# Attention, a 2-D Fourier mix and a feed-forward net on one core: the second feature chunk is made 97 wide, and the last 64 keys are weighed in four 64x64 tiles

## The chip, the core and the metric

The program runs on one core of a Trainium2 chip. It works on five engines: TensorE (PE in the profile, with its weight loads as PEld), VectorE (DVE), ScalarE (ACT), GpSimd (POOL), and SyncE (SP), whose queue issues the DMAs. The metric is the device time of one execution in microseconds.

## The reference

Attention over 4 batches, 12 heads, 448 tokens and 64 features a head, with a soft cap; then the real part of a 2-D Fourier transform over tokens and features is added; then a layer norm and a two-layer net of 768 to 3072 to 768.

```
scores = scale * q @ k.T;  scores = cap * tanh(scores / cap)
attn   = exp(scores - max) / (sum + 1e-9);  x = attn @ v        # heads side by side: 4 x 448 x 768
u      = x + real(fft(fft(x, axis=1), axis=2))
un     = (u - mean(u)) / sqrt(var(u) + 1e-6)
out    = u + maximum(un @ w_ch1, 0) @ w_ch2
```

Everything is computed with the accuracy of 32-bit floats. Operands of the net and of the scores are split into a head and a rest, so that each product is three matmuls of the type fp32r. The products with the values `v` and the transform use plain 32-bit matmuls. In the trace a plain 32-bit matmul is two records, and an fp32r matmul is one.

## The kernel before

**Attention** goes by pairs of heads: 6 pairs in each of 4 batches, 24 in all. The 448 keys of a pair are cut into 7 units: three chunks of 128 keys for head 0, three for head 1, and one unit that holds the last 64 keys of head 0 on partitions 0 to 63 and the last 64 keys of head 1 on partitions 64 to 127. I call that one the shared unit. It is the last unit of an even pair and the first of an odd one (`chunk`, L366), so there are 24 shared units among 168, and two of them always meet at the border of two pairs.

Two units make a tile `t`. `scores` (L398) computes k times q for both units, keys on the partitions and 452 query columns, into one of two PSUM tiles. The units of one head use 64 rows of the array, and those of the other head use the other 64. `tanh` and `exp` (L413, L417) run on ACT over 128x904 elements, from PSUM into one of five SBUF tiles `a`.

`weigh` (L423) multiplies the exponentials with the values. Queries stand in four groups of 112 to 114, and each group is cut at 64, so a unit of one head is 8 matmuls: keys on 128 rows, 64 or 50 query columns as the stationary operand, and 65 moving columns (64 features and a column of ones that gives the denominator). For the shared unit the moving operand is 130 wide: `vt` holds two chunks for it (numbers 7 and 8) with head 0's values beside zeros and zeros beside head 1's. PSUM tile `av` has two banks. Groups 0 and 1 are in the first, groups 2 and 3 in the second. There is one `av` tile only, so a pair's first `weigh` waits until DVE has read the pair before it (`denominators`, `normalise`, L445 and L454).

**The transform** of a batch runs when its six pairs are there. DVE folds the tokens and the features. 193 folded features remain; they are cut into 97 and 96 (`FW`, L55). `stage1` (L498) transforms over tokens: for each feature chunk `p` and each half `sd` 8 matmuls, whose stationary operand has 64 columns and then 33 (`p` = 0) or 32 (`p` = 1), and whose output goes to partitions 0 to 63 and from 64 on. `combine` copies on ACT and adds on DVE into `y`. `stage2` (L528) transforms over features, with 97 or 96 rows.

**The net** takes the 24 groups of 128 hidden channels two by two: `up` (L739) and `down` (L762), all on TensorE with 448 columns, three matmuls for each product.

**What sets the order.** Every step has a place in a table (`ORDER`, L91), and the steps are recorded in that order. Each engine runs its own steps strictly so. The table interleaves the attention of later pairs with the transform of earlier batches. The net can't begin in full before the last `tanh`, whose PSUM tiles it takes over (L955 to L959).

## Time and profile before

| what | value |
|---|---|
| time, median of 3 runs | 955.84 us (955.51 to 956.01) |
| the profiled execution's own time | 956.33 us |
| its span, first to last instruction | 954.1 us |
| PE busy | 939.2 us, 98% |
| DVE busy | 733.6 us, 77% |
| ACT busy | 362.3 us, 38% |
| granted TensorE clock | 1.000 |

The 2.2 us between the span and the execution's own time lie around the program. The profiled execution is 0.49 us above the median. A page of the profile gives busy shares over the whole span; since the first quarter (attention and transform) and the rest (the net) are different programs, the shares have to be read by stage. Busy time of PE counts a matmul from its start to a modelled end, and such records overlap, so the pitch from one start to the next is the cost of a matmul and not its mean duration.

### The profile page before, as it was taken

The page shows a single profiled execution, that of the slowest core. Times are in us where ns is not written, and L with a number is a line of the kernel's source. Part 1 is how long each engine was busy: PE and PEld are TensorE (multiplying, and loading weights), DVE is VectorE, ACT ScalarE, POOL GpSimd, SP SyncE. Part 2 cuts the span into 40 slices and gives each one's busy share as a digit, 9 for nine tenths or more (in the row PEclk, how much of TensorE's full clock was granted, in tenths as well). Part 3 has the DMA queues.
Part 4 walks back from the last instruction along what each step waited for, and adds up shares of the span by engine and source line. Part 5 has one row for each costly group of instructions (what it writes and reads, how often), then busy time and mean ns, then how long its engine had stood idle before and what let it go on. Part 6 is the DMA issues. An engine that isn't in the chain of part 4 may idle for free.

```text
span 954.1 us, 17612 instructions
## 1 busy us (share of the span) xinstructions
PE 939.2 (98%) x7264; PEld 834.5 (87%) x7264; DVE 733.6 (77%) x1486; ACT 362.3 (38%) x563; POOL 16.5 (2%) x50
## 2 busy tenths in 40 slices
PE   6999999999999999999999999999999999999998
PEld 5888788787888999999999999999999999999997
DVE  3589887798988887887877878778777777777733
ACT  6998989995431312222122221221212221122100
POOL 0000101000100000000000000000000000000000
PEclk9999999999999999999999999999999999999999
DMA  5454332420021222111221212111211121112023
GB/s 158 124 172 137 103 106 50 126 49 19 11 76 34 67 60 59 58 60 50 62 65 50 60 50 64 53 50 52 64 50 50 50 67 50 50 51 64 18 108 124
DMA packets 51055, 66.17 MB, mean 69 GB/s; under 512 B 30752, under 2 KB 35616, under 8 KB 50976
## 3 DMA queue, kind: packets, MB, share of 16 engines
q1 hardware_dynamic: 50896, 64.81, 22.8%
q8 instruction: 57, 0.93, 0.4%
q10 hardware_dynamic: 80, 0.25, 0.1%
q14 instruction: 22, 0.18, 0.1%
HBM read 59.53 MB, written 5.52 MB: 68 GB/s over the span
## 4 chain that ended last, share of the span: by engine, by line
PE 95%; DVE 2%; ACT 1%; DMA 1%; issue 1%; SPq 0%; DVEq 0%
PE ph L747 37%; PE po L776 36%; PE av L436 9%; PE s L405 7%; PE yps L506 3%; PE pq L534 2%; PE pt L621 1%; DMA qkr<-qkT 1%; ACT a L415 1%; ACT a L418 0%; DVE xc L737 0%; DVE xc L785 0%; ACT hh L758 0%; DVE hh L759 0%; DVE bs L567 0%
## 5 line engine op out<-in xcount | busy, mean ns | idle before, releaser
L776 PE MATMUL po<-hh,w 128*128 128x448 f32 x1728 | 361.8, 367 | 1.8 <-DVE xc L785 1.4
L747 PE MATMUL ph<-xs,w 128*128 128x448 f32 x1728 | 359.3, 366 | 0.0
L776 PEld LDWEIGHTS po<-hh,w 128*128 128x128 f32 x1728 | 323.0, 188 | 34.2 <-DVE xc L785 5.1
L747 PEld LDWEIGHTS ph<-xs,w 128*128 128x128 f32 x1728 | 323.9, 188 | 27.8 <-issue 0.6
L785 DVE TENSOR_TENSOR xc<-xc,po 128x448 f32<-128x448 f32 x288 | 176.7, 618 | 44.4 <-PE po L776 43.9
L666 ACT ACTIVATE wt<-raw 128x384 f32<-128x384 f32 x96 | 53.5, 557 | 243.7 <-DVE w L698 242.4
L759 DVE SCALAR_TENSOR_TENSOR hh<-ph,hh 128x448 fp32r<-128x448 f32 x96 | 60.0, 625 | 96.7 <-ACT hh L758 96.5
L758 ACT ACTIVATE hh<-ph 128x448 fp32r<-128x448 f32 x96 | 52.3, 544 | 170.4 <-PE ph L747 170.4
L436 PEld LDWEIGHTS av<-vt,a 128*50 128x50 f32 (+1 forms) x2688 | 91.4, 131 | 12.4 <-issue 9.1
L436 PE MATMUL av<-vt,a 128*64 128x65 f32 (+3 forms) x2688 | 98.8, 230 | 0.3 <-PE rt L590 0.3
L310 ACT CAST w<-wt 128x384 fp32r<-128x384 f32 x96 | 49.3, 514 | 130.2 <-DVE wt L673 130.2
L418 ACT ACTIVATE a<-a,capt 128x904 f32<-128x904 f32 x84 | 86.1, 1063 | 0.6
L405 PE MATMUL s<-qhl,khl 64*128 64x452 f32 (+1 forms) x504 | 78.1, 400 | 8.2 <-DVE khl L315 7.6
L415 ACT ACTIVATE a<-s,tscale 128x904 f32<-128x904 f32 x84 | 83.5, 1022 | 7.0 <-PE s L405 5.8
L405 PEld LDWEIGHTS s<-qhl,khl 64*128 64x128 f32 (+1 forms) x504 | 51.7, 193 | 21.9 <-DVE khl L315 7.6
L673 DVE SCALAR_TENSOR_TENSOR wt<-wt 128x384 f32<-128x384 f32 x96 | 53.6, 559 | 10.8 <-DVE wt L670 0.9
L670 DVE SCALAR_TENSOR_TENSOR wt<-raw,wt 128x384 uint32<-128x384 uint32 x96 | 53.7, 559 | 3.3
L692 DVE SCALAR_TENSOR_TENSOR wt<-raw,wt 128x384 f32<-128x384 uint32 x96 | 53.6, 558 | 3.3
L698 DVE TENSOR_TENSOR w<-wt 128x384 fp32r<-128x384 f32 x96 | 53.6, 558 | 3.3
L315 DVE TENSOR_TENSOR wt<-wt,w 128x384 f32<-128x384 f32 x96 | 52.9, 551 | 0.7 <-ACT w L310 0.7
L667 DVE TENSOR_SCALAR wt<-raw 128x384 uint32<-128x384 uint32 x96 | 34.2, 356 | 1.3
L689 DVE TENSOR_SCALAR wt<-wt 128x384 uint32<-128x384 uint32 x96 | 34.0, 354 | 0.4
(61 smaller groups left out, 399.5 us busy)
## 6 DMA issues: line engine op xcount, KB each, us to landing
raw<-w2r SPq DMA_DIRECT2D x48, 384.0 KB
raw<-w1r SPq DMA_DIRECT2D x48, 384.0 KB
qkr<-qkT SPq DMA_DIRECT2D x23, 482.0 KB
vt<-vr SPq DMA_DIRECT2D x24, 288.0 KB
outT<-xc SPq DMA_DIRECT2D x24, 224.0 KB
dev<-lnrow SPq DMA_DIRECT2D x4, 224.0 KB
mean<-lnrow SPq DMA_DIRECT2D x4, 224.0 KB
featT<-feat SPq DMA_DIRECT2D x2, 386.0 KB
```

The costliest lines, as they stand in the source:

```text
L405: nc.tensor.matmul(ps_t[t][:, i, :SQ], khl[p % 2][rows, ik, k0 : k0 + P], qhl[p % 2][rows, iq], start=(k_ == 0), stop=(k_ == 2),)
L415: nc.scalar.activation(a_t[t], ps_t.pop(t)[:, :, :SQ], AF.Tanh, scale=tscale)
L418: nc.scalar.activation(a_t[t], a_t[t], AF.Exp, scale=capt)
L436: nc.tensor.matmul(pa_t[p][q0:q1, g // 2, o : o + n_ * (D + 1)], a_t[t][:, n, OFF[g] + q0 : OFF[g] + q1], v, start=u % 7 == 0 and g % 2 == ...
L670: nc.vector.scalar_tensor_tensor(tu, hi.bitcast(U32), 0xC0000000, tu, op0=ALU.bitwise_and, op1=ALU.bitwise_or)
L673: nc.vector.scalar_tensor_tensor(t, w, HI_MIN, t, op0=ALU.is_ge, op1=mul)
L692: nc.vector.scalar_tensor_tensor(w, lo, 2.0**-52, w, op0=mul, op1=mul)
L698: nc.vector.tensor_tensor(ws[c][1][:, sl], t, w, op=add)
L747: nc.tensor.matmul(ph[:, :S], w_[:, dc * P : (dc + 1) * P], x_, start=(k_ == 0), stop=(k_ == 3 * NDC - 1),)
L759: nc.vector.scalar_tensor_tensor(hh[:, 1], ph[:, :S], 0.0, f32(hh[:, 0]), op0=ALU.max, op1=sub)
L776: nc.tensor.matmul(po[:, :S], w_[:, dc * P : (dc + 1) * P], hh[:, x_], start=(k_ == 0), stop=(k_ == 3 * GF - 1),)
L785: nc.vector.tensor_tensor(ac, ac, po[:, :S], op=add)
```

## The change

The feature chunks are both 97 wide. The second starts at feature 96 rather than 97, so feature 96 is in both, and the constant `feat` has zeros for it in the second chunk. `stage1` has 33 columns in its upper half for both chunks, and `combine` and `stage2` work on 97 partitions for both.

The shared unit is weighed head by head. The stationary operand is the head's 64 rows, 64 or 50 columns, and the moving operand is 65 columns of one chunk of `vt` (number 6), of which partitions 0 to 63 belong to head 0 and the others to head 1. That makes 16 matmuls in place of 8. Each head has a PSUM bank of `av` with its four query groups, and the reads of `denominators` and `normalise` follow it. `vt` has 7 chunks in place of 9, so its load is 7/9 as large and three small memsets go.

```
-FW = (NF // 2 + 1, NF // 2)
+FW = NF // 2 + 1
...
-        for p, w in enumerate(FW):
-            d = (p * FW[0] + np.arange(w))[:, None]
-            half = np.where(d == NF - 1, 0.5, 1.0)
+        for p in range(2):
+            d = (p * (NF - FW) + np.arange(FW))[:, None]
+            half = np.where(d == NF - 1, 0.5, 1.0) * np.where((d == NF - FW) & (p == 1), 0.0, 1.0)
...
-    vt = new([P, 2, 9, D + 1], F32, "vt", 1, "vt")
+    vt = new([P, 2, 7, D + 1], F32, "vt", 1, "vt")
...
-        i, n_ = {None: (7, 2), 0: (c + (c > 0), 1), 1: (4 + c, 1)}[head]
-        v = vt[:, p % 2, i : i + n_].rearrange("q a c -> q (a c)")
+        i = 6 if head is None else 3 * head + c
+        first, last = ((0, 1), (6, 6)) if p % 2 == 0 else ((0, 0), (5, 6))
         for g in range(4):
-            o = (g % 2 * 2 + (head or 0)) * (D + 1)
-            for q0, q1 in ((0, D), (D, R)):
-                nc.tensor.matmul(
-                    pa_t[p][q0:q1, g // 2, o : o + n_ * (D + 1)],
-                    a_t[t][:, n, OFF[g] + q0 : OFF[g] + q1],
-                    v,
-                    start=u % 7 == 0 and g % 2 == 0,
-                    stop=u % 7 == 6 and g % 2 == 1,
+            for j in (0, 1) if head is None else (head,):
+                rows = slice(P) if head is not None else slice(j * D, (j + 1) * D)
+                for q0, q1 in ((0, D), (D, R)):
+                    nc.tensor.matmul(
+                        pa_t[p][q0:q1, j, g * (D + 1) : (g + 1) * (D + 1)],
+                        a_t[t][rows, n, OFF[g] + q0 : OFF[g] + q1],
+                        vt[rows, p % 2, i],
+                        start=u % 7 == first[j] and g == 0,
+                        stop=u % 7 == last[j] and g == 3,
...
-        f, p0, w = f_t[b, sd], p * FW[0], FW[p]
+        f, p0 = f_t[b, sd], p * (NF - FW)
...
-                for q0, q1 in ((0, D), (D, w)):
+                for q0, q1 in ((0, D), (D, FW)):
```

The order of the steps is untouched. What changes in TensorE's row of instructions is seen at the end of pair 5, where a shared unit is followed by the first `stage1` of a second chunk (`p` = 1, half 0 of batch 0), then scores, then the shared unit of pair 6. In the rows, `av` is the tile of `weigh`, `yps` that of `stage1` and `s` that of `scores`, and the sizes are stationary by moving columns. Before:

```order
L436 MATMUL av<-vt,a 50x65
L436 MATMUL av<-vt,a 64x130
L436 MATMUL av<-vt,a 50x130
...
L506 MATMUL yps<-seqT,ff 64x113
L506 MATMUL yps<-seqT,ff 32x113
...
L405 MATMUL s<-qhl,khl 128x452 x12
```

The same place on TensorE in the changed kernel:

```order
L434 MATMUL av<-vt,a 64x65
L434 MATMUL av<-vt,a 50x65
...
L504 MATMUL yps<-seqT,ff 64x113
L504 MATMUL yps<-seqT,ff 33x113
...
L402 MATMUL s<-qhl,khl 128x452 x12
```

Nothing stands in another place. The shared unit's 8 rows with 130 columns are 16 rows with 65, and the 8 rows of `stage1` end on 33 columns and no longer on 32.

## Rows read from the trace of the kernel before

**Rows 1.** The page, part 4: the chain that ended last, shares by engine and line.

```profile
PE 95%; DVE 2%; ACT 1%; DMA 1%; issue 1%; SPq 0%; DVEq 0%
PE ph L747 37%; PE po L776 36%; PE av L436 9%; PE s L405 7%; PE yps L506 3%; PE pq L534 2%; PE pt L621 1%; DMA qkr<-qkT 1%; ACT a L415 1%; ACT a L418 0%; DVE xc L737 0%; DVE xc L785 0%; ACT hh L758 0%; DVE hh L759 0%; DVE bs L567 0%
```

**Rows 2.** Busy time of each engine by stretch: attention, last transform, net.

```profile
core 0: us, PE busy (x) PEld busy (x) DVE busy (x) ACT busy (x) POOL busy (x), PEclk, DMA share, GB/s
...
20.00:225.60 205.60, 204.93 (x3525) 168.35 (x3521) 167.32 (x379) 195.33 (x248) 11.62 (x30) 1.00 0.37 104
225.60:300.00 74.40, 71.88 (x425) 60.07 (x426) 63.47 (x126) 24.05 (x47) 3.85 (x10) 1.00 0.10 34
300.00:954.00 654.00, 650.50 (x3186) 596.96 (x3185) 496.37 (x965) 130.99 (x254) 0.00 (x0) 1.00 0.20 59
```

**Rows 3.** Waits of ACT, 20 to 225.6: for whom, total us, times, longest.

```profile
ACT a L415 <- PE s L405: 4.4, 8, 1.4
ACT yh L310 <- PE yps L506: 2.9, 5, 1.3
ACT a L415 <- PE av L436: 1.1, 4, 0.3
ACT khl L310 <- PE s L405: 0.5, 2, 0.3
ACT xc L310 <- PE pt L621: 0.3, 1, 0.3
```

**Rows 4.** PE in order of time, both chunks' `stage1`: start, us, instructions.

```profile
61.70 0.99 PE L506 MATMUL yps<-seqT,ff 112*64 112x113 f32 x16
62.51 2.02 PE L436 MATMUL av<-vt,a 128*50 128x65 f32 x48
64.36 2.61 PE L506 MATMUL yps<-seqT,ff 112*64 112x113 f32 x16
66.91 1.50 PE L405 MATMUL s<-qhl,khl 64*128 64x452 f32 x12
```

**Rows 5.** PE in order of time: `weigh` alone, and with a shared unit.

```profile
24.55 3.01 PE L436 MATMUL av<-vt,a 128*64 128x65 f32 x96
...
152.06 2.08 PE L436 MATMUL av<-vt,a 128*64 128x65 f32 x64
...
205.12 3.90 PE L436 MATMUL av<-vt,a 128*64 128x130 f32 x112
```

**Rows 6.** PE in order of time: scores of two heads, one tile.

```profile
216.01 0.88 PE L405 MATMUL s<-qhl,khl 64*128 64x452 f32 x6
```

**Rows 7.** Forms of `weigh` on PE, all of the span: busy us, mean ns.

```profile
L436 PE MATMUL av<-vt,a 128*64 128x65 f32 x1152 | 75.4, 224 | 0.0
L436 PE MATMUL av<-vt,a 128*64 128x130 f32 x192 | 26.0, 277 | 0.3 <-PE rt L590 0.3
```

**Rows 8.** ACT in order of time around its longest waits (in brackets).

```profile
86.46 1.01 ACT L415 ACTIVATE a<-s,tscale 128x904 f32<-128x904 f32 x1 [1.35 <-PE s L405]
87.38 1.98 ACT L418 ACTIVATE a<-a,capt 128x904 f32<-128x904 f32 x2
...
90.80 1.05 ACT L418 ACTIVATE a<-a,capt 128x904 f32<-128x904 f32 x1
...
121.88 0.59 ACT L310 COPY yh<-yps 96x226 f32<-96x226 f32 x2 [1.29 <-PE yps L506]
...
134.95 1.02 ACT L415 ACTIVATE a<-s,tscale 128x904 f32<-128x904 f32 x1 [0.57 <-PE s L405]
...
147.34 1.01 ACT L415 ACTIVATE a<-s,tscale 128x904 f32<-128x904 f32 x1 [0.79 <-PE s L405]
...
190.95 0.35 ACT L310 COPY yh<-yps 97x226 f32<-97x226 f32 x1 [0.70 <-PE yps L506]
```

**Rows 9.** All engines in order of time: the last pair and the last batch's `stage1`.

```profile
217.49 3.87 PE L436 MATMUL av<-vt,a 128*64 128x130 f32 x112 [0.30 <-PE rt L590]
...
221.42 0.23 DVE L451 TENSOR_SCALAR den<-av,guard 114x8 f32<-114x8 f32 x1 [0.46 <-PE av L436]
...
226.36 0.56 DVE L491 TENSOR_TENSOR ff<-tf 114x386 f32<-114x386 f32 x1
...
227.37 1.03 DVE L491 TENSOR_TENSOR ff<-tf 114x386 f32<-114x386 f32 x2
...
228.38 0.34 ACT L310 COPY yh<-yps 96x226 f32<-96x226 f32 x1 [2.40 <-PE yps L506]
...
228.76 1.77 DVE L526 TENSOR_TENSOR y<-yps,yh 96x226 f32<-96x226 f32 x4 [0.35 <-ACT yh L310]
...
229.71 3.59 PE L506 MATMUL yps<-seqT,ff 112*64 112x113 f32 x32 [0.45 <-ACT yh L310]
...
233.38 0.34 ACT L310 COPY yh<-yps 96x226 f32<-96x226 f32 x1 [1.80 <-issue]
233.76 0.81 DVE L526 TENSOR_TENSOR y<-yps,yh 96x226 f32<-96x226 f32 x2 [1.78 <-ACT yh L310]
...
234.63 1.85 PE L534 MATMUL pq<-featT,y 96*64 96x192 f32 x20 [0.20 <-DVE y L526]
```

More of the change, by code (lines that the diff above doesn't have):

```diff
@@ L256, in _dft_constants @@
     for n, f in enumerate((np.cos, np.sin)):
-        for p, w in enumerate(FW):
-            d = (p * FW[0] + np.arange(w))[:, None]
-            half = np.where(d == NF - 1, 0.5, 1.0)
-            feat[n, :w, p, NJO : NJO + len(j_even)] = half * f(2 * np.pi * ((d * j_even) % DM) / DM)
-            feat[n, :w, p, :NJO] = half * f(2 * np.pi * ((d * j_odd) % DM) / DM)
+        for p in range(2):
+            d = (p * (NF - FW) + np.arange(FW))[:, None]
+            half = np.where(d == NF - 1, 0.5, 1.0) * np.where((d == NF - FW) & (p == 1), 0.0, 1.0)
+            feat[n, :FW, p, NJO : NJO + len(j_even)] = half * f(2 * np.pi * ((d * j_even) % DM) / DM)
+            feat[n, :FW, p, :NJO] = half * f(2 * np.pi * ((d * j_odd) % DM) / DM)
     ks = np.array(KODD + KEVEN)
@@ L429, in weigh @@
             pa_t[p] = psum.tile([P, 2, 512], F32, tag="av", bufs=1, name="av")
-        i, n_ = {None: (7, 2), 0: (c + (c > 0), 1), 1: (4 + c, 1)}[head]
-        v = vt[:, p % 2, i : i + n_].rearrange("q a c -> q (a c)")
+        i = 6 if head is None else 3 * head + c
+        first, last = ((0, 1), (6, 6)) if p % 2 == 0 else ((0, 0), (5, 6))
         for g in range(4):
-            o = (g % 2 * 2 + (head or 0)) * (D + 1)
-            for q0, q1 in ((0, D), (D, R)):
-                nc.tensor.matmul(
-                    pa_t[p][q0:q1, g // 2, o : o + n_ * (D + 1)],
-                    a_t[t][:, n, OFF[g] + q0 : OFF[g] + q1],
-                    v,
-                    start=u % 7 == 0 and g % 2 == 0,
-                    stop=u % 7 == 6 and g % 2 == 1,
-                    skip_group_check=True,
-                )
+            for j in (0, 1) if head is None else (head,):
[7 more added lines that the diff above has]
+                        stop=u % 7 == last[j] and g == 3,
+                        skip_group_check=True,
+                    )
     def denominators(p):
@@ L448, in denominators @@
             u_t[b] = new([P, 4, DM], F32, f"x{b % 2}", 1, "u")
-        pa = pa_t[p][:R, :, : 4 * (D + 1)].rearrange("q a (g c) -> q a g c", g=4)
+        pa = pa_t[p][:R, :, : 4 * (D + 1)].rearrange("q j (g c) -> q j g c", g=4)
         den = den_t[p] = new([P, 2, 4, 1], F32, "den", 2, "den")
@@ L455, in normalise @@
         b, c0 = p // NP, PAIRS[p % NP] * 2 * D
-        pa = pa_t[p][:R, i, : 4 * (D + 1)].rearrange("q (g j c) -> q g j c", g=2, j=2)
-        den = den_t[p][:R, i].rearrange("q (g j) c -> q g j c", g=2)
+        pa = pa_t[p][:R, :, : 4 * (D + 1)].rearrange("q j (g c) -> q g j c", g=4)[:, 2 * i : 2 * i + 2]
+        den = den_t[p][:R, :, 2 * i : 2 * i + 2].rearrange("q j g c -> q g j c")
         nc.vector.tensor_tensor(
             u_t[b][:R, 2 * i : 2 * i + 2, c0 : c0 + 2 * D].rearrange("q g (j c) -> q g j c", j=2),
-            pa[:, :, :, :D],
+            pa[..., :D],
             den.to_broadcast([R, 2, 2, D]),
@@ L518, in combine @@
             y_t[b, p] = new([P, 2, 2 * NT2], F32, "y", 2, "y")
-        y, w = y_t[b, p][: FW[p], sd], FW[p]
-        ps = d_t.pop(("y", b, p, sd))[:w, : 4 * NK].rearrange("w (n e m) -> w n e m", n=2, e=2)
-        half = new([P, 2, NK], F32, "yh", 2, "yh")[:w]
+        y = y_t[b, p][:FW, sd]
+        ps = d_t.pop(("y", b, p, sd))[:FW, : 4 * NK].rearrange("w (n e m) -> w n e m", n=2, e=2)
+        half = new([P, 2, NK], F32, "yh", 2, "yh")[:FW]
         copy("combine", b, half, ps[:, :, 1])
@@ L531, in stage2 @@
         for sd, (j0, nj) in enumerate(SDJ):
-            for p, w in enumerate(FW):
+            for p in range(2):
                 for q0, q1 in ((0, D), (D, R)):
@@ L535, in stage2 @@
                         ps[q0:q1, j0 : j0 + nj],
-                        y_t[b, p][:w, sd, k0 + q0 : k0 + q1],
-                        featT[n][:w, p, j0 : j0 + nj],
+                        y_t[b, p][:FW, sd, k0 + q0 : k0 + q1],
+                        featT[n][:FW, p, j0 : j0 + nj],
                         start=(p == 0),
@@ L973 @@
         qk[:, :, j, :, SQ + P :] = kj[..., : 3 * P]
-    vr = np.zeros((B, NP, P, 9, D), np.float32)
-    chunks = v[:, :, : 3 * P].reshape(B, NP, 6, P, D).transpose(0, 1, 3, 2, 4)
-    vr[:, :, :, 0], vr[:, :, :, 2:7] = chunks[:, :, :, 0], chunks[:, :, :, 1:]
+    vr = np.zeros((B, NP, P, 7, D), np.float32)
+    vr[:, :, :, :6] = v[:, :, : 3 * P].reshape(B, NP, 6, P, D).transpose(0, 1, 3, 2, 4)
     for j in range(2):
-        vr[:, :, j * D : (j + 1) * D, 7 + j] = v[:, j::2, 3 * P :]
+        vr[:, :, j * D : (j + 1) * D, 6] = v[:, j::2, 3 * P :]
     arrays = {
```

3 lines of the change are left out of this document (removed).

## Prediction

> **What bounds the kernel now.** The chain that ended last comes first: 95% of it is PE, with the net's two lines at 73% [rows 1]. The table by stage then tells which part of the program the change can reach. From 300 us on, PE is busy 650.5 of 654 us with `up` and `down`, which the diff doesn't touch [rows 2]. So every gain has to be made before, and is then carried to the end as a shift of the net. From 20 to 225.6 us (attention with the transforms of batches 0 to 2), PE is busy 204.9 of 205.6 us, but ACT is busy 195.3 too [rows 2]. Two engines are nearly full at once, and a saving on PE is worth no more than what ACT loses by waiting for PE. The share of ACT over the whole span, 38%, hides this.
>
> ACT's waits in that stretch are all for PE and sum to 9.2 us in 20 waits (4.4, 2.9, 1.1, 0.5 and 0.3) [rows 3]. Each also costs the overlap of two instructions: two exps in a row take 1.98 us and one alone 1.05, so the second adds 0.93, and 0.12 is lost when ACT has to start afresh [rows 8]. Twenty times 0.1 is 2.0. **ACT's bound is therefore 9.2 + 2.0 = 11.2 us** for the stretch. From 225.6 to 300 us the last batch's transform has chains of its own, below.
>
> **Part 1: 33 columns in place of 32.** The first chunk's `stage1` takes from 61.70 to 62.51 us, 0.81, and the second chunk's from 64.36 to 66.91, 2.55 [rows 4]. Both are 16 records over the same 113 moving columns, and the second has one stationary column fewer. In the first chunk the blocks of 64 and of 33 columns stream side by side in two halves of the array, 8 records each, so one takes 0.81/8 = 0.10 us. One after the other 16 records would take 1.62 us. The second chunk needs 0.93 more than that, and what is left to explain it is that a block of 32 columns is a narrower strip of the array than one of 64, and that the array empties when the strips change: 8 changes in 8 matmuls, 0.93/8 = 0.12 us each. With 33 columns both blocks are of the wider kind, as in the first chunk. Eight such steps (4 batches, 2 halves) save 8 x 1.74 = 13.9 us on PE; six of them, 10.4 us, lie before 225.6 us. The extra row that `combine` and `stage2` get is no extra column for ACT or DVE, and I cost it at nothing: DVE's and ACT's time goes by columns, and `stage2` rows of 97 already stand beside those of 96.
>
> **Part 2: the shared unit.** `weigh` costs (3.01 - 2.08)/32 = 0.029 us a record with 65 columns, from 96 and 64 records, so 0.47 us for a unit of 16 [rows 5]. Six such units and a shared one take 3.90 us, which puts the shared unit at 3.90 - 3.01 = 0.89 [rows 5]. It has 16 records of twice the columns; a record is modelled at 277 ns against 224 [rows 7]. After the change it has 32 records of 65 columns on four tiles of the array. The trace of before shows no fp32 matmul on half of the rows, so I bound it. At best the four tiles stream side by side, and the unit costs what 8 records in each of four tiles cost: 0.47. At worst they share what two tiles have now: 32 x 0.029 = 0.93. The nearest row is the scores: six matmuls, three in each half of the rows, with 452 columns take 0.88 us, and twelve take 1.50, so two of them cost 0.21, about what 452 columns take at one a cycle of 2.4 GHz (0.19) with the clock granted in full [rows 2, 4, 6]. Two halves of the rows do run side by side there, and I take 0.47.
>
> To that come changes between tiles of 128 rows and of 64. Where a shared unit borders on scores there was a change already; where it borders on `weigh`, `stage1` or `stage2` there is a new one. In the program's order I count 26 for 24 units, at 0.12 each: 0.13 a unit. So the unit goes from 0.89 to 0.60, and 23 units (one lies before 20 us) save 23 x 0.29 = 6.7 us.
>
> The Trainium skill, in "TensorE: Matmul & The Clock Gate", section "Wait — 56ns, not 53.3ns?", says that matmuls never start less than some 25 ns apart, however few columns they have. By it 32 records would take an estimated 0.80 us, and with the changes 0.93, so this part would save nothing. The trace has no stretch of `weigh` denser than the 29 ns above, so it doesn't decide; this is the second rival.
>
> The load of `vt` is 7/9 as large; no row of PE waits for it in this stretch, so nothing. `denominators` and `normalise` read the same number of elements from two banks; a read of PSUM that got dearer would lie behind PE's wait for `av`, but I see no reason for it.
>
> **What of it arrives.** PE saves 10.4 + 6.7 = 17.1 us before 225.6, and ACT can gain 11.2. So ACT becomes the bound, and the question is which of its waits close. The five longest make 4.70 of the 9.2 us [rows 8]. The two for `combine` (1.29 and 0.70) stand right behind second-chunk `stage1` and close whole: 1.99. The one at 86.46 (1.35) follows 5 us of `stage2`, `weigh` and scores that don't shrink, and PE's lead from earlier savings is limited by the two PSUM tiles of scores; I give it 1.0. Ahead of those at 134.95 and 147.34 (0.57, 0.79) only shared units shrink, one and two of them: 0.3 + 0.6. Together 3.89 of 4.70, 83%. The same share of 11.2 us is **9.3 us**.
>
> **The end of attention.** The last two pairs' `weigh` each hold a shared unit, and DVE waits for them: at 221.42 for 0.46 us [rows 9]. Each is 0.3 us shorter: **0.6 us**.
>
> **The last batch's `stage1`** stands alone on the chain. The first (second chunk) has its second half's input at 226.36 + 0.56 = 226.92 and its result is copied at 228.38 [rows 9]. Four matmuls, two by two, need 4 records of 0.10 us in each half of the array, so this half would end at 227.4. But the add that follows finds DVE busy with the other fold until 227.37 + 1.03 = 228.40, so it starts at 228.40 and not 228.76: 0.36 is won. The third `stage1` starts when that add has freed its PSUM tile, 229.71 - 0.36 = 229.35, and ends by 230.3 (0.9 later). The fourth, second chunk again, then takes 0.9 us in place of 2.55 and is copied at some 231.25 in place of 233.38. Its adds end at 232.5 (behind the third's, which end at 231.6), against 233.76 + 0.81 = 234.57. `stage2`, at 234.63 on the path, goes on at 232.5 [rows 9]. **2.1 us** of the 3.5 that PE saves.
>
> Behind that PE and DVE go on with the same work, all of it shifted. Sum: 9.3 + 0.6 + 2.1 = **12.0 us**. The profiled execution took 956.33 us, so it would take 944.3; it is 0.49 above the median, and I predict **943.8 us**.
>
> **The rivals.**
>
> *Half of ACT's waits stay.* The order was laid out for PE as slow as it is, and when PE is early it waits for an exp, or for DVE to read the one `av` tile, and ACT then waits for PE's answer. That DVE waits for `av` and PE for DVE in turn speaks for it; that so many waits stand behind work that shrinks by more than they last speaks against it. Half of 11.2 is 5.6: 5.6 + 0.6 + 2.1 = 8.3 us, 947.5.
>
> *The shared unit gains nothing* (four tiles get the issue rate of two, the page's rule above). It would cost 0.93 + 0.13 = 1.06, and 23 of them 3.9 us more than now. PE then saves 10.4 - 3.9 = 6.5 us in the stretch, all of it below ACT's bound; at 83% 5.4 us, nothing at the end of attention, and 2.1: 7.5 us, 948.3.
>
> *Slower: halves of the rows empty the array.* If going from head 0's rows to head 1's costs what a change of strip costs in the second chunk's `stage1` (0.12), the unit has 8 such changes and no overlap of the halves: 0.93 + 0.13 + 8 x 0.12 = 2.0 us, 1.1 above now, and the 23 cost 25.3 us against 10.4 saved. PE, which is full, ends attention 14.9 us later; with 2.1 won after it the kernel takes 968.6. It decides from about 0.54 us more a unit ((10.4 + 2.1)/23). Against it stand the scores, which change halves at every matmul and still overlap [rows 6]. The Trainium skill, "TensorEngine Tiling (Array Packing)", section "Key Properties", says that a change of mode drains TensorE and a change of tile within a mode doesn't; by that this rival is out, and the scores agree.
>
> *ACT isn't the bound* and all of PE's saving arrives: 17.1 + 0.6 + 2.1 = 19.8, 936.0. ACT's busy time speaks against it.
>
> **How the numbers follow.** Chances: the forecast 0.60, half of the waits 0.18, no gain in the shared unit 0.14, slower 0.04, the full saving 0.04. The range is made of the first three. At the fast end all of ACT's 11.2, 0.6, the 2.1 with half a microsecond more, and some 1.5 for waits too short to be listed: 15.9, 939.9, say 939.5. At the slow end the two rivals together: half of 6.5, and 2.1, which is 5.4: 950.4, say 950.5. Faster by over 0.2% (about what a measurement of this kernel can tell from no change) has 0.95, within it 0.01, slower 0.04.
>
> **What the profile of the changed kernel would show.** Every `stage1` of 16 records at 0.8 us; if a second chunk still takes over 2, part 1 is wrong. A shared unit at 0.5 to 0.6 us between its neighbours; 0.9 or more means the second rival. ACT's waits for PE before the last exp down from 9.2 to 2 or 3 us, and visible waits of PE for ACT in their place, which there are hardly any of now; if ACT's waits stay at 5, the first rival. The net's part (from its first full `up` to the end) unchanged within 1 us; if it grew, the shift was lost to DVE or to the weights' loads there, and the prediction is wrong in its last step.

## The result, and the profile after

The changed kernel takes **947.62 us** (median of 5 runs, 945.25 to 950.13) against 955.84 (954.55 to 956.10) for the kernel before on the same chip: a ratio of 0.9916, with a 95% interval of 0.9895 to 0.9938. It is 8.2 us faster; 943.8 and a gain of 12.0 had been forecast. Two things stand out before any row is read. The gain is two thirds of the forecast, and the five runs lie 4.9 us apart where the five of before lay 1.6 apart. The profiled execution took 947.62 us, its span 945.5.

The page's chain that ended last, shares by engine and line, answers [rows 1]:

```profile
PE 83%; ACT 7%; DVE 7%; issue 2%; DMA 0%; POOL 0%; SPq 0%; DVEq 0%; ACTq 0%; POOLq 0%
PE ph L745 37%; PE po L774 37%; PE av L434 4%; PE s L402 3%; ACT a L412 3%; ACT a L415 2%; PE pq L532 2%; DVE y L524 1%; ACT u L610 1%; DVE bs L565 1%; DVE u L456 1%; DMA capt<-cap 0%; ACT xc L310 0%; ACT khl L310 0%; DVE tf L475 0%
```

PE had 95% of the chain and has 83%. The net's two lines are where they were (74%); it is attention that has changed hands, with 7% each for ACT and DVE. The table by stage, for the stretches that answer [rows 2] (each stage begins some 6 to 8 us sooner):

```profile
core 0: us, PE busy (x) PEld busy (x) DVE busy (x) ACT busy (x) POOL busy (x), PEclk, DMA share, GB/s
20.00:219.70 199.70, 190.33 (x3870) 156.17 (x3868) 165.61 (x376) 192.88 (x246) 12.40 (x30) 1.00 0.34 100
219.70:292.20 72.50, 68.35 (x428) 59.25 (x427) 63.31 (x127) 24.29 (x48) 3.83 (x10) 1.00 0.11 35
292.20:945.50 653.30, 649.73 (x3186) 596.74 (x3184) 496.00 (x965) 131.17 (x254) 0.00 (x0) 1.00 0.19 59
```

PE's busy time in attention fell from 204.9 to 190.3 us, and 9.4 us of the stretch are now idle on PE, where 0.7 were. The work was taken off TensorE as planned; a good part of what was taken off became TensorE's waiting. The net is unchanged (649.7 us of PE's time against 650.5).

The waits of ACT in that stretch (whom for, us in total, times, longest), against [rows 3]:

```profile
ACT a L412 <- PE s L402: 2.7, 4, 0.8
ACT wt L664 <- DVE w L696: 1.3, 2, 1.0
ACT a L412 <- PE av L434: 0.9, 2, 0.6
ACT khl L310 <- PE s L402: 0.5, 2, 0.3
ACT yh L310 <- PE yps L504: 0.4, 1, 0.4
ACT xc L310 <- PE pt L619: 0.3, 1, 0.3
```

They sum to 6.1 us, 4.8 of it for PE, where 9.2 stood. Half of ACT's waits for PE stayed, which the prediction had named as the sign of its first rival.

What the two parts do to the instructions themselves is in PE's order of time (start, us, instructions). First both chunks' `stage1`, against [rows 4]:

```profile
62.04 0.99 PE L504 MATMUL yps<-seqT,ff 112*64 112x113 f32 x16
62.85 1.73 PE L434 MATMUL av<-vt,a 128*50 128x65 f32 x64
64.52 0.99 PE L504 MATMUL yps<-seqT,ff 112*64 112x113 f32 x16
65.44 0.88 PE L402 MATMUL s<-qhl,khl 64*128 64x452 f32 x6
```

The first chunk takes 0.81 us to the next instruction, the second 0.92, where it took 2.55. Then the shared unit, alone between scores and `stage2`:

```profile
85.66 0.69 PE L434 MATMUL av<-vt,a 64*64 64x65 f32 x32
86.28 2.83 PE L532 MATMUL pq<-featT,y 97*64 97x194 f32 x32
```

It has 32 records and takes 0.62 us (85.66 to 86.28). 0.60 was forecast; the unit of before, at this same place, took 0.95 (86.97 to 87.92). 0.62 us for 32 records is 19 ns a record. The Trainium skill, in "TensorE: Matmul & The Clock Gate", section "Wait — 56ns, not 53.3ns?", says that matmuls never start less than some 25 ns apart; here, with four tiles of the array in use, they do, and the trace decides.

One row of the changed kernel has no answer in the kernel before:

```profile
51.93 1.15 PE L434 MATMUL av<-vt,a 128*64 128x65 f32 x31
54.80 1.62 PE L434 MATMUL av<-vt,a 128*50 128x65 f32 x49 [1.72 <-issue]
```

In the middle of a `weigh` of 80 records TensorE stands for 1.7 us and waits for no semaphore. Until 54 us this execution was 1.5 us ahead of the profile of before; behind the stop it is 0.3 behind, by VectorE's instructions. Then the lead builds up anew, to 1.9 at 92 us, 3.8 at 156, 5.9 at 222 and 7.9 at 300 (the same instruction's start in both traces, on ACT or DVE); at 600 us it is 8.2.

So three questions go to the chip: what the stop is, what the spread is, and why half of ACT's waits stay although PE has 14.6 us less to do.

### The profile page after: what moved, and what is told of

Same layout as the page of the kernel before. It is cut to its first block, busy times and chain, and to the rows that moved or that the text cites. A ratio compares the mean times of both kernels' runs of the same rounds, so it can differ in the third digit from the quotient of the medians.

```text
span 945.5 us, 18375 instructions
## 1 busy us (share of the span) xinstructions
PE 920.4 (97%) x7648; PEld 821.2 (87%) x7648; DVE 732.4 (77%) x1486; ACT 361.5 (38%) x563; POOL 17.0 (2%) x47
## 4 chain that ended last, share of the span: by engine, by line
PE 83%; ACT 7%; DVE 7%; issue 2%; DMA 0%; POOL 0%; SPq 0%; DVEq 0%; ACTq 0%; POOLq 0%
PE ph L745 37%; PE po L774 37%; PE av L434 4%; PE s L402 3%; ACT a L412 3%; ACT a L415 2%; PE pq L532 2%; DVE y L524 1%; ACT u L610 1%; DVE bs L565 1%; DVE u L456 1%; DMA capt<-cap 0%; ACT xc L310 0%; ACT khl L310 0%; DVE tf L475 0%
## 5 line engine op out<-in xcount | busy, mean ns | idle before, releaser
L434 PEld LDWEIGHTS av<-vt,a 128*50 128x50 f32 (+3 forms) x3072 | 84.4, 130 | 18.3 <-issue 11.0
L434 PE MATMUL av<-vt,a 128*50 128x65 f32 (+3 forms) x3072 | 92.0, 223 | 4.0 <-issue 1.7
L402 PE MATMUL s<-qhl,khl 64*128 64x452 f32 (+1 forms) x504 | 78.5, 399 | 11.2 <-DVE khl L315 8.5
```

Of the source, the lines that this page charges most:

```text
L402: nc.tensor.matmul(ps_t[t][:, i, :SQ], khl[p % 2][rows, ik, k0 : k0 + P], qhl[p % 2][rows, iq], start=(k_ == 0), stop=(k_ == 2),)
L434: nc.tensor.matmul(pa_t[p][q0:q1, j, g * (D + 1) : (g + 1) * (D + 1)], a_t[t][rows, n, OFF[g] + q0 : OFF[g] + q1], vt[rows, p % 2, i], sta ...
```

## Experiments

Twelve more runs follow, the first of them of the changed kernel itself. Each was timed beside the kernel before on the same chip, but not all twelve on one chip; the edits are to the changed kernel unless said otherwise.

**The changed kernel again** (`e1_again`, no edit), to see whether the stop comes again.

> The changed kernel once more, word for word. In its first trace TensorE stands still for 1.9 us at 54.8 us in the middle of a weigh, with no semaphore to wait for, and all the lead it had by then (1.5 us) is gone. Theory A (its instructions came late, because their load stood behind a burst of other DMAs from 48.7 us on): the stop is there again, at the same instruction, with 1 to 2.5 us. Rival (a chance event): no stop there, and the profiled execution is 1.5 to 2 us shorter. Time of the whole: 945 to 950 us either way.

Measured: 948.32 us (946.28 to 949.87), ratio 0.9928 (0.9914 to 0.9942). Its profile has no stop at this place:

```profile
53.29 2.55 PE L434 MATMUL av<-vt,a 128*64 128x65 f32 x80
```

The same 80 records run through in 2.55 us. So the stop is no property of the order alone; it comes in some executions. Both expectations miss: there is no stop, and yet this execution is no shorter. Two things cost it what the stop cost the other. Its first `weigh` started at 15.06 us and not at 13.87. Even so it is 0.5 us ahead of the changed kernel's first profile from 92 to 219 us; then it loses 1.0 us in the last batch's transform, where the granted TensorE clock is not 1.00 but half of that (columns as in the table by stage above):

```profile
223.20:226.60 3.40, 3.40 (x38) 2.95 (x36) 1.29 (x4) 1.16 (x3) 0.00 (x0) 0.51 0.00 0
```

0.5 is 1.2 GHz where 1.00 is 2.4. TensorE had waited 0.7 and 0.9 us for DVE just ahead of it (from 220.0 and 222.0 us on); the changed kernel's first profile has the same two waits and stays at 1.00. So there is scatter at the start, and scatter by the clock.

**Part 1 alone** (`e2_chunk97`: chunks 97 wide, the shared unit as before) and **part 2 alone** (`e3_shared`: the four tiles, chunks of 97 and 96 as before), each cut to the line that decides:

```
e2:  ...
     -            for j in (0, 1) if head is None else (head,):
     +            o = (g % 2 * 2 + (head or 0)) * (D + 1)
     ...
e3:  -FW = NF // 2 + 1
     +FW = (NF // 2 + 1, NF // 2)
     ...
```

> Only the first part of the change: both feature chunks 97 wide, the shared unit as before. Theory A (TensorE's saving arrives only as far as ScalarE and VectorE leave room, so the parts overlap): 6 to 7 us faster than before, 949 to 950, of which 2.1 come after 225 us in the last batch; the two parts alone sum to more than the 8.2 us of both. Rival (TensorE is the bound all along, savings add up): 13.9 of the 20.6 us that TensorE saves, so 5.5 us, 950.3, and the sum of the parts is 8.2.

> Only the second part: the shared unit in 64x64 tiles with its PSUM layout, feature chunks 97 and 96 as before. A shared unit takes 0.6 us instead of 0.9 in any case. Theory A: 3.5 to 4.5 us faster than before, 951.5 to 952.3, nothing of it in the last batch after 225 us. Rival (savings add up): 6.7 of 20.6, so 2.7 us, 953.1. Either way a second chunk's stage1 takes 2.5 us again.

Measured: part 1 alone 949.34 us, ratio 0.9945 (0.9932 to 0.9957), 5.6 us less than before, the rival's figure. Part 2 alone 954.31, ratio 0.9995 (0.9985 to 1.0005): nothing, and both expectations miss (3.5 to 4.5 and 2.7 us). The sum, 6.3, is neither expectation's (8.2 or more); it is close to the 6.7 us that both give together on this chip (`e1_again`), so nothing here shows that the two compete for the same ACT waits. What takes part 2's gain stands in its profile, which is of a run of 956.00 us, 1.7 above its median. Between 39 and 56 us PE has three such stops, of which the last is:

```profile
52.72 1.15 PE L434 MATMUL av<-vt,a 128*64 128x65 f32 x31
55.87 2.69 PE L434 MATMUL av<-vt,a 128*50 128x65 f32 x49 [2.00 <-issue]
...
56.10:59.50 3.40, 3.40 (x51) 3.18 (x48) 0.81 (x4) 1.54 (x2) 0.00 (x0) 0.50 0.39 145
```

From one start to the next the three are 1.1, 0.5 and 2.2 us long, together more than the part wins where they are missing (2.1 us, below). Right behind the last one the granted clock is 0.50 for 3.4 us (the last row, columns as in the table by stage), so the 49 records take 2.6 us to the next instruction where they take 1.5 behind the changed kernel's stop.

**A thinner burst of loads** (`e4_thin`): two loads of weights and one of constants moved away from 50 us, since the stop of the changed kernel fell into such a burst.

```
-        5, 119, 190, 191, 242, ...      "fetch"
+        5, 119, 203, 213, 242, ...
-        287, 150, 196, 189              "load_constant"
+        287, 150, 286, 189
```

> The changed kernel with three loads moved out of the burst at 49 to 52 us: two raw weight blocks (places 190 and 191 of the order to 203 and 213) and the second feature constant (196 to 286). Theory A (late instructions behind that burst): the stop at 54.8 us is gone or under 0.3 us, the lead over before at 56 us is 1.5 us and more instead of none, and the whole is 1 to 2 us shorter than the changed kernel, 945.6 to 946.6. Rival (the stop has another cause): it is still there, and the time is the same within 0.5 us. If the stop goes but the time stays, VectorE, which is full from 56 to 83 us, has taken it.

Measured: 948.56 us (945.92 to 949.74), ratio 0.9926 (0.9912 to 0.9940). The profiled execution has no stop before 60 us and is the fastest of the six (945.92), but the median is that of the plain repeat and not the 945.6 to 946.6 of theory A. No gain from moving these loads shows.

**VectorE relieved** (`e5_dve`): one conversion of weights moved behind 85 us.

```
-        ..., 269, 273, 280, 286, 422, ...      "weights"
+        ..., 269, 376, 390, 405, 422, ...
-        ..., 242, 295, 370, 475, ...           "fetch"
+        ..., 242, 295, 412, 475, ...
```

> The changed kernel with one conversion of weights (its load and its three steps) moved from the stretch 60 to 85 us to the stretch 85 to 105 us, so that VectorE has about 3.5 us less to do where it is busy 19.1 of 20 us. Theory D (VectorE is the bound there and swallows the savings): the lead over the kernel before, 0.3 us higher at 82 us than at 21 us in the first repeat, becomes 1 to 2 us higher, and the median falls by 1 to 2 us, to 946 or 947. Theory O (the kept order is the bound: ACT has no idle time to give before 64 us, and behind it the engines wait for one another at fixed places): the lead at 82 us moves by under 0.5 us, the moved steps collide with other work later, and the median is 948 to 950.

Measured: 949.51 us (947.65 to 950.51), ratio 0.9940 (0.9927 to 0.9953). VectorE's busy time from 54 to 84 us went from 27.10 to 24.86 us. The stop of 1.9 us comes at 54.6 us as in the changed kernel's profile. Here is one and the same tanh in the kernel before, in the changed kernel and in this one:

```profile
84.12 0.99 ACT L415 ACTIVATE a<-s,tscale 128x904 f32<-128x904 f32 x1
83.66 1.00 ACT L412 ACTIVATE a<-s,tscale 128x904 f32<-128x904 f32 x1
82.23 1.00 ACT L412 ACTIVATE a<-s,tscale 128x904 f32<-128x904 f32 x1
```

The lead over the kernel before is 1.9 us, where the changed kernel has 0.5. Of the 1.4 us between the two, 0.2 were there from the start, and 1.0 is work of ACT itself: the moved conversion has two instructions of some 0.5 us on ACT. At 100 us the lead is 2.6 against 1.9, so about half a microsecond of theory D's gain shows. Then the moved steps are met again, in the rows of VectorE and PE:

```profile
102.90 0.56 DVE L671 SCALAR_TENSOR_TENSOR wt<-wt 128x384 f32<-128x384 f32 x1
103.38 0.42 DVE L456 TENSOR_TENSOR u<-av,den 114x256 f32<-114x256 f32 x1
...
103.89 2.30 PE L434 MATMUL av<-vt,a 64*64 64x65 f32 x83 [1.27 <-issue]
```

They stand between the two halves of `normalise`, and the next pair's `weigh` waits 1.3 us. It starts 0.1 us behind the end of the second half, which has to have read `av`; the view itself names no releaser. At 120 us the lead is 1.3 us, where the changed kernel has 1.9. Theory O's collision and its median came true, its lead at 82 us didn't. Theory D's gain is there in part and is lost again 20 us later. What VectorE does counts here by where it stands, not only by how full the engine is.

**Heads apart** (`e7_apart`): in the shared unit the eight matmuls of head 0 come first, then those of head 1.

```
-        for g in range(4):
-            for j in (0, 1) if head is None else (head,):
+        for j in (0, 1) if head is None else (head,):
+            for g in range(4):
```

> The changed kernel with the shared unit's matmuls in another order: all eight of head 0 (rows 0 to 63), then all eight of head 1 (rows 64 to 127), with the same tiles and the same output. Theory: the two row halves run side by side because neighbouring instructions alternate between them; apart, only two tiles run at a time, the unit goes from 0.62 to about 0.9 us, and with 23 units some 6 us of PE and 3 to 5 us of the time come back: 951 to 953. Rival: what counts is only that the tiles are four and small; the unit stays at 0.6 us and the time at 946 to 950.

Measured: one run of 950.56 us, and in its profile

```profile
86.08 0.97 PE L434 MATMUL av<-vt,a 64*64 64x65 f32 x32
86.97 2.83 PE L532 MATMUL pq<-featT,y 97*64 97x194 f32 x32
```

The unit takes 0.89 us (86.08 to 86.97) instead of 0.62, with the same tiles, sizes and records. The gain of part 2 on TensorE comes from neighbours that stand in different row halves; a head at a time it takes nearly as long as the unit of before (0.95). The time is 2.2 us above the median of the next kernel (`e8_vt`), from the same chip, and just below the 951 to 953 expected; this execution also has a stop (1.6 us at 42.9), so the time of one run says no more than that it doesn't contradict.

**The first V load earlier** (`e8_vt`), for the scatter at the start:

```
-        5, 119, 190, ...      "fetch"
+        11, 119, 190, ...
-        11, 24, 81, ...       "load_v"
+        5, 24, 81, ...
```

> The changed kernel with the first load of V put ahead of the first load of weights (two issues on SP change places in the first 4 us). In the profiles of the kernel before and of the first repeat the first weigh waits for that load until 15.06 us, in three others it starts at 13.9 us. Theory S (this chance at the start makes a good part of the spread of 946 to 950 us): the first weigh starts at 13.9 us or sooner, the runs lie within 2.5 us, and the median is 947.0 to 947.6. Rival: the spread comes from stops of TensorE without a semaphore later on; the runs still lie 3 to 4 us apart and the median stays at 948 to 948.6.

Measured: 948.39 us (945.45 to 951.03), ratio 0.9926 (0.9911 to 0.9941). The first `weigh` starts at 13.44 us, and still the runs lie 5.6 us apart. The start isn't the main part of the spread; the rival's median came true (948 to 948.6), and the runs lie further apart than its 3 to 4 us.

**What the stops have in common.** With nine profiles at hand the stops could be laid side by side. Counted in all of TensorE's records in the trace (matmuls, weight loads and the few semaphore instructions) they don't fall just anywhere: before 60 us they stand ahead of records 1217, 1473 and 1729 (in `e3_shared` all three, in the changed kernel and `e5_dve` the last, in `e7_apart` the first). These are 256 apart. And the page has a queue that carries instructions, q8, with 60 packets of 16 KB (57 in the kernel before); one packet belongs to each 256 records. From the trace's list of packets:

```
kernel        block entered at   its successor's packet starts   first record of the successor     TensorE stands
before            46.08 us             +3.1 us                     4.06 us after that packet           -
after             35.45                +3.1                        2.37                              0.1 us
after             40.88                +4.4                        2.40                              0.2
after             47.70                +4.8                        2.35                              1.9
e1_again          48.73                +0.9                        4.56                                -
e3_shared         35.07                +4.0                        2.45                              1.1
e3_shared         41.50                +4.7                        2.44                              0.5
e3_shared         48.59                +4.6                        2.64                              2.2
```

Half of the packets start within 0.5 us of TensorE's entering the block before, and seven tenths within 1 us (421 packets before 225 us in the fourteen profiles). Where it is 3 to 5 us late in the changed kernel and in `e3_shared`, some 1050 to 1130 packets of loads lie in between, 837 to 896 of them of 256 bytes: a pair's load of V, whose rows of 64 floats stand 65 apart in `vt`. In the kernel before it is 287 packets, none of them V's. And in all fourteen profiles the first record of a block never starts less than 2.2 us after its packet.

Two things differ between the kernels. The first is where a block begins. In the kernel before, V's packets start from 37.70 to 39.11 and from 44.13 to 45.51 us, just ahead of the blocks entered at 39.57 and 46.08, and the profile of part 1 alone (`e2_chunk97`) has no such stop either. The 16 further records and 16 further weight loads of each shared unit, 768 in all, begin the blocks elsewhere: in the changed kernel at 35.45, 40.88 and 47.70, and V's loads (35.96 to 37.26, 42.80 to 44.13, from 51.19 on) come ahead of the packet. Not in every execution: in the profile of `e4_thin`, with the same loads of V, these three packets start within 0.5 us and ahead of V's. The second is how long a block lasts. The blocks entered at 39.57 and 46.08 us in the kernel before lasted 6.5 and 7.2 us; those entered at 35.45, 40.88 and 47.70 in the changed kernel last 5.4, 6.8 and, without the stop, 5.2. So a packet 3 us late came in time for the slower TensorE, and one 4.8 us late doesn't for the faster. The DMA view of the changed kernel from 47.71 to 52.40 us and from 52.40 to 54.80 (queue, packets, MB, share) shows the late one:

```profile
q1 hardware_dynamic: 1032, 0.84, 61.3%
...
q8 instruction: 1, 0.02, 2.8%
```

**V in wide rows.** This can be tried without touching TensorE: let V stand 65 wide in memory, with the column of ones, so that a partition's part of a load is one run of 1820 bytes; the memset of that column goes. The changed kernel (`e9_wide`), the kernel before (`e10_before_wide`, nine chunks, with the zeros where they are) and part 2 alone (`e11_shared_wide`) were given the same edit:

```
-        nc.sync.dma_start(vt[:, p % 2, :, :D], vr[p // NP, PAIRS[p % NP]])
+        nc.sync.dma_start(vt[:, p % 2], vr[p // NP, PAIRS[p % NP]])
...
-    vr = np.zeros((B, NP, P, 7, D), np.float32)
+    vr = np.ones((B, NP, P, 7, D + 1), np.float32)
...
```

> The changed kernel with V laid out in memory 65 wide, the column of ones with it, so that a pair's load is 128 packets of 1820 bytes instead of 896 of 256. Theory I (TensorE's next 16 KB of instructions come late because their packet waits behind a V load's 896 packets: in the changed kernel's profile it starts 3.1, 4.4 and 4.8 us after TensorE has entered the block before, and the third time TensorE stands for 1.9 us; the shortest from packet to first instruction is 2.3 us): no packet starts over 2 us late, no stop without a semaphore up to 220 us, the first weigh doesn't wait for its V either, the runs lie within 2 us, and the median falls by 1.5 to 3 us to 945.3 to 947.0. Rival: the stops and the spread have another cause; the median stays at 948 to 949 and the runs 3 to 4 us apart.

> The kernel before with V laid out 65 wide in the same way (nine chunks, 128 packets of 2340 bytes instead of 1152 of 256). Theory I: TensorE takes 6.5 to 7 us for a block of instructions there, a packet 3.1 us late still comes in time, so nothing but the first weigh's wait can go: 0 to 1.2 us less, 953.8 to 955. Against the same edit in the changed kernel this gives what the change is worth without the stops: 8.3 to 9.3 us. Rival (the wide load is better in itself, by fewer packets): 2 to 3 us less here too, 952 to 953.

> The shared unit's four tiles alone (features still in chunks of 112 and 82) with V laid out 65 wide. With the narrow loads this part gained nothing (ratio 0.9995), and its profile had three stops of TensorE of 3.8 us in all. Theory I: the stops go and the part is worth 1.0 to 2.5 us against the kernel before, 952.5 to 954. Rival (the part has no worth: ACT and VectorE are the bound where it saves): 954.3 to 955.5.

Measured (median, lowest to highest, number of runs; ratio to the kernel before with narrow rows on the same chip):

| kernel | narrow rows of V | wide rows of V |
|---|---|---|
| before | 955.35 (954.48 to 956.60), 21 runs, the chip of the wide ones | 954.72 (954.06 to 955.77), 11 runs, 0.9993 (0.9984 to 1.0002) |
| part 2 alone | 954.31 (952.41 to 957.97), 11 runs, 0.9995 (0.9985 to 1.0005) | 952.58 (951.11 to 954.23), 11 runs, 0.9972 (0.9963 to 0.9981) |
| changed | 948.32 (946.28 to 949.87), 6 runs, 0.9928 (0.9914 to 0.9942) | 947.07 (946.81 to 947.73), 4 runs, 0.9913 (0.9899 to 0.9926) |

The kernel before gains nothing that can be told from no change. Part 2 alone (in chunks of 97 and 96, not the 112 and 82 of its expectation) now gains 2.8 us over the kernel before, and this interval lies clear of the one with narrow rows: that is the evidence for what V's loads cost. The changed kernel's four runs lie 0.9 us apart instead of 3.6 for six; those of part 2 alone still lie 3.1 apart (5.6 before). The place where the changed kernel stood, with wide rows:

```profile
52.31 2.55 PE L433 MATMUL av<-vt,a 128*64 128x65 f32 x80
```

Theory I holds in the main. In two points it doesn't. The median is 947.07, just above its range. And three packets are still 2.6, 3.3 and 3.8 us late, behind some 280, 530 and 430 packets of loads, of which V's are at most 128; the last ends in a stop:

```profile
167.53 2.70 PE L433 MATMUL av<-vt,a 128*64 128x65 f32 x96
171.16 0.87 PE L401 MATMUL s<-qhl,khl 64*128 64x452 f32 x6 [0.93 <-ACT xc L310]
```

The view puts it down to ACT; the packet list has the block's packet at 168.92, 2.24 us ahead of this start, as short as that distance gets anywhere. So it is loads in general that hold an instruction packet up. Narrow rows aren't needed for it: in the profile of `e12_two_terms` below, with wide rows, two packets are 4.7 and 5.0 us late behind 281 and 802 packets of loads, and TensorE stands for 1.3 and 1.7 us. `e9_wide` is faster than the changed kernel by some 1.4 us if the ratios of one and the other are compared (0.9913 and 0.9928), but the intervals overlap, and four runs are few to call it steadier.

What the change is worth without V's narrow rows follows from that table: 954.72 - 947.07 = 7.65 us, less than the 8.3 to 9.3 expected. Part 2 has 954.72 - 952.58 = 2.1 of it and part 1, on top of it, 952.58 - 947.07 = 5.5, much as alone (5.6). That is still only two thirds of 12.0, so V's loads explain a part of the spread and at most a microsecond or two of the median, not the shortfall.

**Is TensorE still the bound?** With wide rows, two more cuts. `e12_two_terms` leaves out a third of the scores' matmuls, one of the three terms, 34 us of TensorE's work; `e13_no_rest_q` takes the subtraction off VectorE that only that third had needed.

```
e12: -        terms = (1, 0), (0, 1), (0, 0)
     +        terms = (1, 0), (0, 0)
     ...
e13: -        minus(qhl[p % 2][:, 1], qk[p][:, :SQ], f32(qhl[p % 2][:, 0]))      (rest_q)
     +        pass
```

> The changed kernel with V 65 wide, and the scores computed from two of their three matmuls (the term of K's high and Q's low part is left out, so the scores are coarser): 168 of 504 scores matmuls at 0.205 us from start to start, 34 us of TensorE's work less before 223 us, ACT's and VectorE's work as it was. Theory H (behind the change the pace before 223 us is set by ACT and VectorE and by what each hands the other by way of TensorE, and TensorE's own work no longer counts): 0 to 1.5 us less than with three terms, 945.5 to 947.1. Rival (the forecast's: ACT's 4.8 us of waits are TensorE's being late): the waits go, 3 to 5 us less, 942 to 944.

> The kernel with two of three scores matmuls, and VectorE's subtraction for Q's low part, which nothing reads any more, left out too: 24 times 0.62 us, 15 us of VectorE's work less. Theory H: 2 to 4 us less than with that subtraction, 942 to 945, since VectorE is full from 54 to 84 us and late at the end of the last batch. Rival (VectorE has room, the pace is ACT's alone or TensorE's): the same as with the subtraction within 1 us.

Measured: 943.54 us (942.87 to 946.52) with two terms and 940.66 (940.37 to 940.79) without the subtraction too. So 34 us off TensorE bring 3.5 us (3.2 by the ratios, since these two were timed on another chip than `e9_wide`), and 15 us off VectorE another 2.9. For the first theory H missed (0 to 1.5) and the rival's number came true (3 to 5), for the second theory H's (2 to 4). The waits of ACT, with V in wide rows (first all three terms, from 20 to 218 us):

```profile
ACT a L411 <- PE s L401: 2.0, 3, 0.8
ACT a L411 <- PE av L433: 0.9, 2, 0.6
ACT xc L310 <- PE pt L618: 0.7, 2, 0.4
ACT khl L310 <- PE s L401: 0.5, 2, 0.3
ACT yh L310 <- PE yps L503: 0.4, 1, 0.4
ACT wt L663 <- DVE w L695: 0.3, 1, 0.3
```

and without the third term and the subtraction, from 20 to 213 us:

```profile
ACT xc L310 <- PE pt L618: 0.3, 1, 0.3
ACT a L411 <- PE s L401: 0.3, 1, 0.3
ACT yh L310 <- PE yps L503: 0.2, 1, 0.2
```

4.8 us have become 0.8, and ACT is busy 191.1 of the 193.0 us: ACT is the bound here, as the forecast had it for the changed kernel. The profile between the two, of `e12_two_terms`, is of its slowest run (946.52), with stops of 1.3 and 1.7 us that end at 50.6 and 57.8 and the clock at 0.50 from 50.8 to 54.2. From 84 to 217 us, behind that, ACT's waits in it sum to 1.5 us, where they sum to 4.2 with all three terms; so the third term alone closes most of them. How the subtraction's 15 us become 2.9 wasn't followed.

## Why the prediction was right, and where it was not

**TensorE's savings** were sized well. Part 1: a second chunk's `stage1` takes 0.92 us where 0.81 was forecast and 2.55 stood. Part 2: 0.62 for the shared unit where 0.60 was forecast; it replaces 0.95 and not 0.89, so 0.33 are saved and not 0.29. The choice between the bounds 0.47 and 0.93 was right for the reason given, as `e7_apart` shows: the row halves run side by side where the order alternates them, and near the dear bound (0.89 measured) where it doesn't. The trace of before spoke against the second rival already: single records of `weigh` start 7 ns apart there (24.549 and 24.556 us, on two tiles), so its 29 ns a record were an average and no floor. With that the rivals in which the shared unit gains nothing, or is slower, are out. So is the one in which all of PE's saving arrives. For part 1 the runs show the price of one column, 2.55 us against 0.92; that the array empties between strips of different width is the forecast's reading of it and wasn't tested apart.

**The last batch's `stage1`**, 2.1 us, held. From the start of its first `stage1` to the second half of `stage2` the wide kernels take 223.85 to 236.08 before and 219.09 to 229.25 after, 12.23 and 10.16 us: 2.07 won. The rows of the changed kernel show the forecast's picture, the third and fourth running through and PE then waiting for DVE:

```profile
221.11 1.38 PE L504 MATMUL yps<-seqT,ff 112*64 112x113 f32 x24 [0.71 <-DVE ff L489]
...
223.42 1.75 PE L504 MATMUL yps<-seqT,ff 112*64 112x113 f32 x32 [0.92 <-DVE y L524]
...
225.83 2.82 PE L532 MATMUL pq<-featT,y 97*64 97x194 f32 x32 [0.66 <-DVE y L524]
```

**The net** carried the shift on, as forecast (650 us of PE's time before and after).

**The step that failed is "83% of ACT's 11.2 us"**, with the 0.6 of the end of attention: 9.9 us up to 222 us. Between the two kernels with wide rows, from 21 to 219 us (the same ACT instruction in both traces), it is 5.3. The 83% came from the five longest waits of [rows 8], 3.89 of 4.70 us. In the changed kernel four of them are met again:

| wait of before | us | forecast to go | after | gone |
|---|---|---|---|---|
| 86.46, tanh for scores | 1.35 | 1.0 | 0.51 | 0.84 |
| 121.88, copy for `stage1` | 1.29 | 1.29 | 0 | 1.29 |
| 134.95, tanh for scores | 0.57 | 0.3 | 0.84 | -0.27 |
| 147.34, tanh for scores | 0.79 | 0.6 | 0.65 | 0.14 |
| 190.95, copy for `stage1` | 0.70 | 0.70 | 0.36 | 0.34 |

2.34 of 4.70 go, 50%, and 0.46 of it come back at once in the tanh's wait for `av` at 190.59, which is 0.65 where 0.19 stood. Over the whole stretch the wide kernels' waits went from 8.7 us to 4.8, so 45% are gone. That is the forecast's first rival, "half of ACT's waits stay", which gave 947.5; 947.62 was measured. That the two lie 0.1 us apart is partly luck, since the measured run had a stop and the repeat on another chip took 948.32, 6.7 us less than before; the share of the waits is the firmer agreement. The rival was given 0.18, since "so many waits stand behind work that shrinks by more than they last". The wait at 134.95 shows why that argument doesn't hold. Here is PE ahead of it in the changed kernel, and ACT behind:

```profile
114.58 1.79 PE L402 MATMUL s<-qhl,khl 64*128 64x452 f32 x12 [0.34 <-ACT a L412]
...
118.72 1.15 PE L434 MATMUL av<-vt,a 128*64 128x65 f32 x32 [0.47 <-ACT a L415]
...
122.89 1.31 PE L619 MATMUL pt<-ident,u 113*128 113x113 f32 x8 [0.61 <-DVE y L524]
...
127.01 3.63 PE L434 MATMUL av<-vt,a 64*64 64x65 f32 x128
...
131.50 1.02 ACT L412 ACTIVATE a<-s,tscale 128x904 f32<-128x904 f32 x1 [0.84 <-PE s L402]
```

PE is early at 114 to 123 us and waits three times, for tanh, for exp and for DVE. What it won is gone by then. From 122.89 it runs 7.7 us of work without a gap in the order laid down, 3.6 of it a `weigh`, before the scores for which ACT waits come up. The wait at 190.95 is a second case. The forecast took it to stand right behind a second chunk's `stage1`, but it is a copy of 97 partitions, of a first chunk: the second chunk's `stage1` ended at 185.67, and scores and 95 records of `weigh` lie in between. In the changed kernel PE comes to those scores early, waits 1.1 us for a tanh, and ACT then waits for the copy's `stage1`:

```profile
180.17 1.51 PE L402 MATMUL s<-qhl,khl 128*128 128x452 f32 x6 [1.12 <-ACT a L412]
...
185.46 0.35 ACT L310 COPY yh<-yps 97x226 f32<-97x226 f32 x1 [0.36 <-PE yps L504]
```

As these two places show it, a saving on PE shortens ACT's wait only if it lies between the last place where PE itself waits for ACT or DVE and the scores in question; savings ahead of that place are given back there. The forecast summed PE's savings from the start of the stretch and took them to be at hand wherever ACT waited. It had named the mechanism, with "when PE is early it waits for an exp, or for DVE", and didn't go through the five waits with it.

The last two experiments agree: taking 34 us more off TensorE everywhere, also between those places, closes most of ACT's waits that were left and is worth 3.5 us. The rule itself is read from the rows and no experiment moved a saving from one side of such a place to the other; which share of the 4.8 us a different order of the steps could win wasn't tried.

**What no step of the prediction had** are the late instruction packets. They go with part 2's worth of nothing when alone (0.9995 with V's narrow rows, 0.9972 with wide ones), and they cost the changed kernel at most one or two microseconds at the median; the range took that in without naming it. Of the spread between runs they are a part. The clock is another: eleven of the runs have a mean granted clock of 0.998, the slowest of six different kernels among them, and none of the kernel before; in the three profiles that show it, it is one stretch of 3.4 us at half clock, behind a stop or behind waits of TensorE. In `e1_again` that stretch cost 1.0 us. The first `weigh`'s start (13.1 to 15.1 us in the profiles) is a third. How much each has of the 5 us was not separated, and part 1 alone, with no stop in its profile, has runs 3.3 us apart.

## What to carry to other kernels

Where two engines hand work to and fro in a fixed order, follow a saving from the instruction that got shorter to the next place at which its own engine waits for the other: up to there it counts, behind it it is lost. A sum of one engine's savings against a sum of the other's waits is only the upper bound. And where a change gives an engine more instructions, or lets it run through them faster, look whether they reach it in time: a load that was harmless before can stop it afterwards, and the time to see it by is the distance from an instruction packet to the first instruction that it brings.

## What was not expected of the hardware

- TensorE stands still for 0.5 to 2.2 us with no semaphore to wait for, at multiples of 256 records, when the 16 KB packet with its next instructions starts later than about 2.3 us before they are due; in fourteen profiles no block began less than 2.2 us after its packet.
- Such a packet starts within 0.5 us of the block before being entered in half of 421 cases, and up to 5 us later when loads lie ahead of it (some 1100 packets, most of 256 bytes, or 281 of mostly 3856 bytes).
- Right behind two of the stops (of 1.3 us in `e12_two_terms` and 2.2 in `e3_shared`) the granted clock was 0.50 for 3.4 us; behind others, of 1.6 to 1.9 us, it stayed at 1.00.
- Records of fp32 matmuls with 64 rows and 65 columns on four tiles take 19 ns each when neighbours alternate between the halves of the rows, and 28 ns (0.89 us for 32) when they do not.
